# Values sorted as rows and regrouped through DRAM, and one batch's queries turned by the DMA crossbar, in a fused attention and feed-forward kernel

## The chip, the cores and the metric

The kernel runs on one core of a Trainium2 chip. The metric is the device time of one launch in microseconds (us), as a median over runs. TensorE is called PE in the profile, its weight loads PEld, VectorE DVE, ScalarE ACT, GpSimd POOL and SyncE SP. SP computes nothing here: its instructions issue DMAs, and they leave in program order, so an SP instruction that waits holds back every one behind it.

## The reference

Inputs are q, k, v of shape (4 batches, 8 heads, 768 tokens, 64), a block-sorting matrix `sort_net` of (4, 8, 8, 8), two feed-forward weights of 512 x 2048 and 2048 x 512, and two scalars.

```python
P = sort_net
for _ in range(5):
    P = exp(P - max(P)); P /= sum(P, -1) + 1e-9; P /= sum(P, -2) + 1e-9
k_sorted = einsum('bhij,bhjcd->bhicd', P, k_blocks)   # 8 blocks of 96 tokens
v_sorted = einsum('bhij,bhjcd->bhicd', P, v_blocks)
attn = softmax(q_blocks @ k_sorted.T / 8)             # 96 x 96 within each block
x = (attn @ v_sorted) laid out as tokens x 512
h = x @ w_in;  r = relu(h);  out = (s * r * r + b) @ w_out
```

The last division of the Sinkhorn loop is folded into the weights that the kernel builds, and `b` into a bias row.

## The kernel before, in words

The work is cut into eight tiles `t` of 384 tokens, two for each batch `b` (t = 2b and 2b+1). For a tile, `ffn1(t)` makes the hidden layer in eight parts, each of eight products of 384 columns (line L448), a Relu on ACT (L460) and a square on DVE (L461). `ffn2(t)` makes three output tiles, each of sixteen products of 512 columns (L472), scaled and biased on DVE (L493) and stored by SP (L496). This is nearly all of PE's time.

The attention of batch n = b+1 is put between these products in a written order: `ffn1` and `ffn2` take a dictionary of slots, and after part i, or after each four products of an output tile, the pieces in that slot are issued. The schedule is manual, so each engine runs its instructions in program order. The pieces of a batch are, with the names of the lines' helpers:

- `build_pd` (`PDB`): one small product and five DVE operations make PD, the 128 x 128 sorting weights, with a row for each (head, block, half block).
- `k_piece` (`K`): 32 products of 64 columns each sort 16 of 48 key columns into KS (L301).
- `v_piece` (`V`): the same for values. It needs a copy VP of the raw values with the order of token and head dimension exchanged, which `v_sort` makes on POOL in eight copies (L198). Each of four pieces has 32 products of 64 columns (L323), with the slices of VP as weights, and an eviction on DVE or ACT into VS (L204, L206). VS holds a token of a half block on each partition and is what the attention product reads.
- queries: batch 0 and batch 1 are loaded as 64-partition rows (`load_qh`), and turned by transposes on PE (`q_trans`, L217, 48 for a half, evicted by `q_evac`). Batches 2 and 3 are loaded by token (`load_q_rows`, eight DMAs on POOL's queue, L115) and turned by two DMA transposes on SP (`q_dma`, L431).
- `s_piece` (`SC`): scores of four blocks and two heads (L355) and the exponential (L363). The first ones of batch n stand after the first four products of `ffn2(2b+1)`.
- `p_piece` (`P`): the attention product (L397) and its scaling (L403). `t_dma` (`TD`): a DMA transpose on SP to the next tile's input (L423).

Batch 0 goes first on its own path, and the change leaves it alone. The pieces of batch 1 stand in `ffn1(1)`, `ffn2(0)` and `ffn2(1)`, those of batch 2 in `ffn1(2)`, `ffn2(2)` and `ffn2(3)`, and so on. Raw tiles of keys, values and queries have two buffers each. POOL loads the next batch with `load_rest(n)`: six DMAs each of keys and values and eight of queries. `load_rest(2)` is queued on POOL behind `v_sort(1)`; `load_rest(3)` waits, by a one-column copy (L89), for the turned queries of batch 2.

Of the kernel before, what the change touches and what calls it, by code (L numbers as in the profile page):

```python
# [22 lines left out]
def kernel(  # L23
# [40 lines left out]
    xtp = ctx.enter_context(tc.tile_pool(name="xtp", bufs=4))  # L64
    rtp = ctx.enter_context(tc.tile_pool(name="rtp", bufs=3))
    gtp = ctx.enter_context(tc.tile_pool(name="gtp", bufs=2))
    osb = ctx.enter_context(tc.tile_pool(name="osb", bufs=3))
    psa = ctx.enter_context(tc.tile_pool(name="psa", bufs=3, space=bass.MemoryType.PSUM))
    psb = ctx.enter_context(tc.tile_pool(name="psb", bufs=2, space=bass.MemoryType.PSUM))
# [39 lines left out]
    def load_q_rows(b):  # L109

        ti = rawp.tile([BLK, NB, H, D], BF, tag="rawq", name="qtok")
        qv = q[b].rearrange("h (n t) d -> t n h d", n=NB)
        for n in range(0, NB, 2):
            for h in range(2):
                nc.gpsimd.dma_start(out=ti[:, n + h], in_=qv[:, n + h])  # L115
        QTOK[b] = ti

    zeros = const.tile([128, 512], BF)
    nc.vector.memset(zeros, 0.0)  # L119
    VP = [const.tile([128, D, GAP], BF, name=f"vp{i}") for i in range(2)]  # L120
    KS = [const.tile([128, NG, 2, GAP], BF, name=f"ks{i}") for i in range(2)]
    VS = [const.tile([KR, 2 * NG, VW], BF, name=f"vs{i}") for i in range(2)]
    nc.vector.memset(VP[0][:, :, C2:GAP], 0.0)
    nc.vector.memset(KS[0][:, :, :, C2:GAP], 0.0)
    dummy = const.tile([128, 1], FP)
    nc.scalar.activation(out=dummy, in_=zeros[:, 0:1], func=AF.Exp)
# [41 lines left out]
        for a in range(NHP):  # L168
            load_wi(c * W4, (c + 1) * W4, slice(a, a + 1))
    nc.gpsimd.memset(ones, 1.0)  # L170
    nc.gpsimd.memset(VP[1][:, :, C2:GAP], 0.0)
    nc.gpsimd.memset(KS[1][:, :, :, C2:GAP], 0.0)
    fill_vs(1)
    for t, src in ((s_bc, moe_s), (b_bc, moe_b)):
# [3 lines left out]
        nc.gpsimd.dma_start(out=wo[:, fs, :], in_=wov[:, fs, :])  # L178
    for t in "vk":
        load(t, 1, 6)  # L180
    for half in range(2):
        load_qh(1, half)

    rstat = const.tile([BH, NB], FP)
    rrec = const.tile([BH, NB], FP)
# [4 lines left out]
    idv = ident.rearrange("p (a e j z) -> p a e j z", a=NHP, e=2, j=NB)  # L190

    def permute(eng, b, src, cs=slice(0, C2), ds=slice(0, D)):
        o = VP[b % 2][:, ds, cs]
        i = src[:, cs, ds].rearrange("p c d -> p d c")
        if eng is nc.scalar:
            eng.copy(out=o, in_=i)  # L196
        else:
            eng.tensor_copy(out=o, in_=i)  # L198
# [9 lines left out]
    def q_trans(b, half):  # L208
        if b not in QT:
            QT[b] = trp.tile([128, 2, NHP, CQ, 64], BF, tag="qt", name="qt")  # L210
        tr = psa.tile([128, 2, 1024], BF, tag="a", name="tqa")
        pr = slice(half * 64, (half + 1) * 64)
        for a in range(NHP):
            for c in range(CQ):
                for e in range(2):
                    o = (a % 2 * CQ + c) * 64
                    nc.tensor.transpose(out=tr[e * 64:(e + 1) * 64, a // 2, o:o + 64],  # L217
                                        in_=QH[b][pr, 2 * a + e, c, :], identity=ident[pr, pr])
        return tr

    def q_banks(b, half, engs):
        if b not in QT:
# [2 lines left out]
        for u in range(2):  # L225
            tr = psb.tile([128, 1024], BF, tag="b", name="tqb")
            for a in range(2 * u, 2 * u + 2):
                for c in range(CQ):
# [8 lines left out]
    def q_evac(b, half, us, eng, tr):  # L237
        evac(eng, QT[b][:, half].rearrange("p (u a) c t -> p u (a c t)", u=2)[:, us],
             tr[:, us, 0:2 * TG])

    idle = [
        lambda: nc.vector.tensor_reduce(
# [48 lines left out]
            in1=spread(pt, [[0, 4 * NHP], list(pt.ap[1])]), op0=ALU.mult, op1=ALU.mult)  # L291
        PD[b] = pd

    def q_half(b, half, eng):
        q_evac(b, half, slice(0, 2), eng, q_trans(b, half))
# [23 lines left out]
    def v_piece(b, d0, eng, halves=None):  # L319
        ps = psa.tile([128, CK, 2 * NG], FP, tag="a", name="tv")  # L320
        for d in range(CK):
            for z in range(2):
                nc.tensor.matmul(out=ps[z * GAP:(z + 1) * GAP, d, :],  # L323
                                 lhsT=VP[b % 2][:, d0 + d, :], rhs=PD[b][:, :, z, :],
                                 start=True, stop=True)
        if halves is None:
            evac(eng, VS[b % 2][:, :, d0:d0 + CK], ps[0:KR].rearrange("p d g -> p g d"))
            return None

        def half(h, eng):  # L330
            hs = slice(h * HB, (h + 1) * HB)
            evac(eng, VS[b % 2].rearrange("p (g i) w -> p g i w", i=NB)[:, :, hs, d0:d0 + CK],
                 ps[0:KR].rearrange("p d (g i) -> p g i d", i=NB)[:, :, hs])

        half(0, eng)
        return lambda eng: half(1, eng)

    AT = {}
    X = {}
# [186 lines left out]
    part(0, 0, (2,))  # L526
    part(0, 1, (2,))

    def v_sort(b, r=range(8)):
        for i in r:  # L530
            permute(nc.gpsimd, b, RAW["v", b], ds=slice(i * 8, (i + 1) * 8))

    scr = const.tile([128, 1], BF)

    def after(ap):
        nc.gpsimd.tensor_copy(out=scr, in_=ap)  # L536
# [24 lines left out]

    def QF0(): return lambda: q_banks(0, 1, "AD")
    def SB(i): return lambda: s_banks(0, 1, i)
    def QF(b, half, eng): return lambda: q_half(b, half, eng)
    def K(b, i, eng): return lambda: k_piece(b, i * CK, eng)
    def V(b, i, eng): return lambda: v_piece(b, i * CK, eng)
    def SC(b, h, i): return lambda: s_piece(b, h, i)
    def P(b, h, i): return lambda: p_piece(b, h, i)
    def TP(b, h, i, eng): return lambda: t_piece(b, h, i, eng)
    def TD(b, h): return lambda: t_dma(b, h)  # L570
    def PDB(b): return lambda: build_pd(b)
    def LD(t, b): return lambda: load(t, b)


    def halves(n):

        if n == 1:
            s0 = {2: [K(n, 0, "D"), K(n, 1, "A"), K(n, 2, "D")],
                  6: [V(n, 0, "D"), V(n, 1, "A"), V(n, 2, "D")],
                  9: [V(n, 3, "A"), QF(n, 0, "D")], 11: [QF(n, 1, "A")]}  # L580
        else:
            s0 = {0: [K(n, 0, "D"), K(n, 1, "A"), K(n, 2, "D")],
                  8: [V(n, 0, "D"), V(n, 1, "A"), V(n, 2, "D")]}
        s1 = {0: [SC(n, 0, 0), SC(n, 0, 1)] if n == 1 else [V(n, 3, "D"), SC(n, 0, 0), SC(n, 0, 1)],
              3: [P(n, 0, 0), SC(n, 0, 2), SC(n, 0, 3)], 4: [P(n, 0, 1)], 5: [P(n, 0, 2)],
              6: [P(n, 0, 3), TD(n, 0), SC(n, 1, 0), SC(n, 1, 1)], 8: [P(n, 1, 0)],
              9: [P(n, 1, 1), SC(n, 1, 2), SC(n, 1, 3)], 10: [P(n, 1, 2)],
              11: [P(n, 1, 3), TD(n, 1)]}
        return s0, s1
# [5 lines left out]
    part(1, 0, (0, 1))  # L595
    t_piece(0, 1, 3, "D")
    part(1, 1, (0, 1))
    ffn1(1, {2: [PDB(1)], 4: [make_bias]}, {0: 2, 1: 2})
    after(GT[1][:, NF - 1, 0:1])
    v_sort(1)  # L600
    load_rest(2)
    s0, s1 = halves(1)
    ffn2(0, s0)
    ffn2(1, s1)
    for b in range(1, B):
        n = b + 1
        s0, s1 = {}, {}
        if n < B:
            if n == 2:
                v_sort(n)  # L610
            q_dma(n)
            if n == 2:
                load_rest(3, QT[2][:, NB - 1, 0, 0:1])
            s0, s1 = halves(n)
        ffn1(2 * b, {4: [PDB(n)]} if 1 < n < B else {})
        ffn1(2 * b + 1, {})
        if n == 3:
            after(GT[2 * b + 1][:, NF - 1, 0:1])
            v_sort(n)
        ffn2(2 * b, s0)  # L620
        ffn2(2 * b + 1, s1)

# [29 lines left out]
```

## Time and profile before

| What | Value |
|---|---|
| median of 3 runs | 230.36 us (229.96 to 230.58) |
| profiled execution: time, span | 232.06 us, 230.3 us |
| PE busy | 219.7 us, 95% of the span, 2690 matmuls recorded |
| DVE, ACT, POOL busy | 120.6, 100.2, 81.8 us |
| products of `ffn1` and `ffn2` (L448, L472, L485) | 86.6, 81.5, 3.7 us busy |
| value sorting on PE (L323), four batches | 10.4 us busy, 512 products |
| query transposes of batch 1 on PE (L217) | 1.9 us busy, 96 |
| permuting copies on POOL (L198) | 19.1 us busy, 24 copies |

A line of the groups names the source line, engine and operation, what is written from what, the shape and the count; then the busy time, the mean of one in ns, and the idle time before the group with what ended it. Matmuls overlap, so that the mean of one (326 ns for 384 columns) is longer than the step from one to the next (86.6 us / 512 = 169 ns). The chain of waits is the path that ended last, followed back from the last instruction; its rows have the start, the length, and what ran.

### The profile page before, as it was taken

The numbers are of one execution on the slowest core, as the hardware profiler recorded it, in microseconds if no ns is written. First come the engines' busy times: TensorE is split into PE (matmuls) and PEld (weight loads), VectorE is DVE, ScalarE is ACT, GpSimd is POOL, SyncE is SP. The second block draws the span as 40 slices with busy tenths as digits, with TensorE's granted clock in tenths as the row PEclk, the third lists the DMA queues.
The fourth block names the chain that finished last, engine by engine and source line by source line (L and its number), as shares of the span: only waits on it lengthen the run. The fifth ranks groups of instructions, "written<-read, shape, count | busy, mean of one in ns | idle before, by whom it ended". The sixth has DMA issues, their size and how long they took to land.

```text
span 230.3 us, 6164 instructions
## 1 busy us (share of the span) xinstructions
PE 219.7 (95%) x2690; PEld 134.4 (58%) x2713; DVE 120.6 (52%) x237; ACT 100.2 (43%) x135; POOL 81.8 (36%) x139
## 2 busy tenths in 40 slices
PE   7978999899999999999999999999999999999994
PEld 5767766456555555666465655565555566554453
DVE  6684457377642774546255765446365664432221
ACT  4785687443215436565015245663033446660000
POOL 7569991267987860469000000005500000000000
PEclk9997999999999999999999999999999999999999
DMA  6999989998199969499912238000111440001112
GB/s 153 277 158 132 128 125 197 205 200 134 51 140 229 179 143 183 73 145 177 110 48 91 70 114 188 0 3 3 66 74 46 117 114 3 1 0 48 72 64 93
DMA packets 45883, 25.05 MB, mean 109 GB/s; under 512 B 29984, under 2 KB 42016, under 8 KB 45856
## 3 DMA queue, kind: packets, MB, share of 16 engines
q0 software_dynamic: 25952, 12.85, 43.9%
q1 hardware_dynamic: 19904, 11.81, 18.5%
q8 instruction: 21, 0.34, 0.6%
q14 instruction: 6, 0.05, 0.1%
HBM read 27.27 MB, written 6.29 MB: 146 GB/s over the span
## 4 chain that ended last, share of the span: by engine, by line
PE 89%; DMA 4%; ACT 2%; issue 2%; SPq 1%; DVE 1%
PE hps L448 37%; PE ops L472 34%; DMA v0f<-in_v_dram 4%; PE tv L323 4%; PE pv L397 4%; PE sc L355 2%; PE tp L301 2%; PE ops L485 2%; PE scb L373 1%; PE tqa L217 1%; PE pv L391 1%; ACT vp L196 1%; SPq L80 1%; PE tr L414 1%; PE pe L276 0%
## 5 line engine op out<-in xcount | busy, mean ns | idle before, releaser
L448 PE MATMUL hps<-xt,wi 128*128 128x384 bf16 x512 | 86.6, 326 | 1.3 <-DVE xt L206 1.3
L472 PE MATMUL ops<-wo,gt 128*128 128x512 bf16 x346 | 81.5, 379 | 2.2 <-issue 1.6
L460 ACT ACTIVATE rt<-hps 128x768 bf16<-128x768 f32 x64 | 51.8, 810 | 39.9 <-PE hps L448 39.3
L448 PEld LDWEIGHTS <-wi 128*128 128x128 bf16 x512 | 48.8, 98 | 33.2 <-issue 1.9
L461 DVE TENSOR_TENSOR gt<-rt 128x768 bf16<-128x768 bf16 x64 | 36.4, 570 | 45.2 <-ACT rt L460 44.9
L472 PEld LDWEIGHTS <-gt 128*128 128x128 bf16 x368 | 33.6, 98 | 36.8
L493 DVE SCALAR_TENSOR_TENSOR ot<-ops,s_bc,bias 128x512 f32<-128x512 f32 (+1 forms) x25 | 18.2, 729 | 36.3 <-PE ops L472 34.1
L403 DVE TENSOR_TENSOR x<-pv,rec 96x512 bf16<-96x512 f32 x32 | 22.0, 687 | 1.1
L363 ACT ACTIVATE at<-sc 112x768 bf16<-112x768 f32 x16 | 12.1, 807 | 21.0 <-PE sc L355 21.0
L198 POOL COPY vp<-rawv 128x384 bf16<-128x384 bf16 x24 | 19.1, 859 | 0.0
L536 POOL COPY scr<-gt 128x1 bf16<-128x1 bf16 x2 | 0.4, 190 | 48.1 <-DVE gt L461 48.0
L397 PEld LDWEIGHTS <-at 112*128 112x128 bf16 (+1 forms) x256 | 13.4, 102 | 6.7 <-ACT at L363 0.6
L204 ACT CAST vs<-tv 112x1024 bf16<-112x1024 f32 (+1 forms) x7 | 6.3, 898 | 23.3 <-PE tv L323 23.2
L206 DVE CAST vs<-tv 112x1024 bf16<-112x1024 f32 (+1 forms) x11 | 12.0, 1122 | 7.3 <-PE tv L323 7.3
L141 POOL DMA_DIRECT2D wi<-in_moe_w_in_dram x24 | 12.9, 566 | 4.7 <-DMA qh<-in_q_dram 2.6
L397 PE MATMUL pv<-vs,at 112*128 112x66 bf16 (+1 forms) x256 | 14.1, 197 | 0.0
L115 POOL DMA_DIRECT2D qtok<-in_q_dram x16 | 12.3, 775 | 2.3 <-PE sc L355 1.0
L92 POOL DMA_DIRECT2D rawk<-in_k_dram x21 | 11.3, 552 | 4.9 <-DMA wo<-in_moe_w_out_dram 4.1
L92 POOL DMA_DIRECT2D rawv<-in_v_dram x18 | 9.7, 578 | 7.7 <-DMA wo<-in_moe_w_out_dram 4.8
L323 PEld LDWEIGHTS <-vp 128*64 128x64 bf16 x512 | 9.4, 117 | 2.9 <-issue 2.1
L131 PE MATMUL z<-zeros 128*64 128x96 bf16 (+2 forms) x129 | 9.8, 242 | 1.3 <-DVE zeros L119 1.2
L206 DVE CAST ks<-tp 128x1024 bf16<-128x1024 f32 x8 | 9.5, 1220 | 2.1 <-PE tp L301 2.0
(83 smaller groups left out, 147.8 us busy)
## 6 DMA issues: line engine op xcount, KB each, us to landing
out_dram<-ot SPq DMA_DIRECT2D x23, 256.0 KB, 2.0
rawv<-in_v_dram POOLq DMA_DIRECT2D x18, 128.0 KB, 6.6
rawk<-in_k_dram POOLq DMA_DIRECT2D x18, 128.0 KB, 5.1
wo<-in_moe_w_out_dram POOLq DMA_DIRECT2D x4, 512.0 KB, 10.4
v0f<-in_v_dram SPq DMA_DIRECT2D x4, 384.0 KB, 7.1
qtok<-in_q_dram POOLq DMA_DIRECT2D x16, 96.0 KB, 4.6
qh<-in_q_dram POOLq DMA_DIRECT2D x3, 384.0 KB, 7.7
wi<-in_moe_w_in_dram POOLq DMA_DIRECT2D x16, 64.0 KB, 3.8
```

The costliest lines, as they stand in the source:

```text
L92: nc.gpsimd.dma_start(out=ti[:, c:c + n, :].rearrange("p c d -> p (c d)"), in_=raw["qkv".index(t)][b][:, c * D:(c + n) * D])
L141: nc.gpsimd.dma_start(out=wi[:, al, f0:f1], in_=wiv[:, al, f0:f1])
L198: eng.tensor_copy(out=o, in_=i)
L206: nc.vector.tensor_copy(out=out, in_=in_)
L323: nc.tensor.matmul(out=ps[z * GAP:(z + 1) * GAP, d, :], lhsT=VP[b % 2][:, d0 + d, :], rhs=PD[b][:, :, z, :], start=True, stop=True)
L397: nc.tensor.matmul(out=pv[0:m, e, n * VW:(n + 1) * VW], lhsT=atf[:, c0:c0 + m], rhs=VS[b % 2][:, e * NG + g0 + n, :], start=True, stop=True)
L403: nc.vector.tensor_tensor(out=x[:, :, hp * 128:(hp + 1) * 128].rearrange("p n (e d) -> p e n d", e=2), in0=pvv[:, :, :, 0:D], in1=rec.unsq ...
L448: nc.tensor.matmul(out=H1[t, i][:, f, 0:TG], lhsT=wi[:, hp, fc:fc + 128], rhs=XT[t][:, :, hp, :], start=(hp == 0), stop=(hp == NHP - 1))
L460: nc.scalar.activation(out=rt, in_=h, func=AF.Relu)
L461: nc.vector.tensor_tensor(out=gt[:, 2 * i:2 * i + 2, :], in0=rt, in1=rt, op=ALU.mult)
L472: nc.tensor.matmul(out=ops, lhsT=gt[:, f, m * 128:(m + 1) * 128], rhs=wo[:, f, :], start=(f == 0), stop=(f == NF - 1))
L493: nc.vector.scalar_tensor_tensor(out=ot[:, ns], in0=ops, scalar=s_bc, in1=BIAS[0][:, ns], op0=ALU.mult, op1=ALU.add)
```

## The change

For batches 1 to 3, the values are sorted as they were loaded: PD is the weight, and the 3072 raw columns (48 tokens x 64) go through in six products of 512 columns (`v_rows`, `VRW`). Each is evicted in place over the raw values by DVE ("D") or ACT ("A"). The sorted rows then have a (parity of head, half block, head pair and block) on each partition and have to be regrouped: `v_back` (`VB`) writes them to DRAM in one DMA (128 rows of 6 KB), and four DMAs read them back into VS in runs of 64 values, one run for each of 48 tokens and 32 groups. All five go through SP's queue. The permuted copies, their buffer VP[1] and the later `v_piece` calls go.

The queries of batch 1 are loaded by token with eight DMAs and turned by two DMA transposes on SP, behind `v_back(1)`. `load_rest(2)` now waits for both of them. PD of batch 1 is built two parts earlier, that of batches 2 and 3 one part earlier. In program order on SP, batch 1 has: a small fill of VS, the write, the four reads, the two query transposes, and then the stores of tile 0; batches 2 and 3 have the two query transposes, the write and four reads, and then the stores of the next tile.

```diff
-    VP = [const.tile([128, D, GAP], BF, name=f"vp{i}") for i in range(2)]
+    VP = const.tile([128, D, GAP], BF, name="vp")
...
-    for half in range(2):
-        load_qh(1, half)
+    load_q_rows(1)
...
+    def v_rows(b, u, eng):
+        w = 512 // D
+        r = RAW["v", b][:, u * w:(u + 1) * w, :].rearrange("p c d -> p (c d)")
+        ps = psb.tile([128, 512], FP, tag="b", name="tvr")
+        nc.tensor.matmul(out=ps, lhsT=PD[b].rearrange("p e z g -> p (e z g)"), rhs=r,
+                         start=True, stop=True)
+        evac(eng, r, ps)
+
+    def v_back(b):
+        vd = drp.tile([2, 2, NG, C2, D], BF, tag="vd", name="vd")
+        nc.sync.dma_start(out=vd.rearrange("e z g c d -> (e z g) (c d)"),
+                          in_=RAW["v", b].rearrange("p c d -> p (c d)"))
+        for z in range(2):
+            for e in range(2):
+                nc.sync.dma_start(
+                    out=VS[b % 2][z * GAP:z * GAP + C2, e * NG:(e + 1) * NG, 0:D],
+                    in_=vd[e, z].rearrange("g c d -> c g d"))
...
-        if n == 1:
-            s0 = {2: [K(n, 0, "D"), K(n, 1, "A"), K(n, 2, "D")],
-                  6: [V(n, 0, "D"), V(n, 1, "A"), V(n, 2, "D")],
-                  9: [V(n, 3, "A"), QF(n, 0, "D")], 11: [QF(n, 1, "A")]}
-        else:
-            s0 = {0: [K(n, 0, "D"), K(n, 1, "A"), K(n, 2, "D")],
-                  8: [V(n, 0, "D"), V(n, 1, "A"), V(n, 2, "D")]}
-        s1 = {0: [SC(n, 0, 0), SC(n, 0, 1)] if n == 1 else [V(n, 3, "D"), SC(n, 0, 0), SC(n, 0, 1)],
+        s0 = {2 if n == 1 else 0: [K(n, 0, "D"), K(n, 1, "A"), K(n, 2, "D")]}
+        s1 = {0: [SC(n, 0, 0), SC(n, 0, 1)],
...
-    ffn1(1, {2: [PDB(1)], 4: [make_bias]}, {0: 2, 1: 2})
-    after(GT[1][:, NF - 1, 0:1])
-    v_sort(1)
-    load_rest(2)
+    ffn1(1, {0: [PDB(1)], 2: [VRW(1, 0, "D")], 3: [VRW(1, 1, "A")], 4: [make_bias, VRW(1, 2, "A")],
+             5: [VRW(1, 3, "D")], 6: [VRW(1, 4, "A")], 7: [VRW(1, 5, "D")]}, {0: 2, 1: 2})
+    nc.sync.dma_start(out=VS[1][C2:GAP, :, 0:D],
+                      in_=spread(zeros[0:GAP - C2, 0:D], [[0, 2 * NG], [1, D]]))
+    v_back(1)
+    q_dma(1)
+    load_rest(2, QT[1][:, NB - 1, 0, 0:1])
...
         if n < B:
-            if n == 2:
-                v_sort(n)
             q_dma(n)
             if n == 2:
                 load_rest(3, QT[2][:, NB - 1, 0, 0:1])
             s0, s1 = halves(n)
-        ffn1(2 * b, {4: [PDB(n)]} if 1 < n < B else {})
-        ffn1(2 * b + 1, {})
-        if n == 3:
-            after(GT[2 * b + 1][:, NF - 1, 0:1])
-            v_sort(n)
+            u0 = {3: [PDB(n)], 5: [VRW(n, 0, "D")], 6: [VRW(n, 1, "D")], 7: [VRW(n, 2, "D")]}
+            u1 = {0: [VRW(n, 3, "D")], 1: [VRW(n, 4, "D")], 2: [VRW(n, 5, "D"), VB(n)]}
+        ffn1(2 * b, u0)
+        ffn1(2 * b + 1, u1)
```

More of the change, by code (lines that the diff above doesn't have):

```diff
@@ L66 @@
     gtp = ctx.enter_context(tc.tile_pool(name="gtp", bufs=2))
+    drp = ctx.enter_context(tc.tile_pool(name="drp", bufs=2, space=bass.MemoryType.DRAM))
     osb = ctx.enter_context(tc.tile_pool(name="osb", bufs=3))
@@ L119 @@
     nc.vector.memset(zeros, 0.0)
-    VP = [const.tile([128, D, GAP], BF, name=f"vp{i}") for i in range(2)]
+    VP = const.tile([128, D, GAP], BF, name="vp")
     KS = [const.tile([128, NG, 2, GAP], BF, name=f"ks{i}") for i in range(2)]
     VS = [const.tile([KR, 2 * NG, VW], BF, name=f"vs{i}") for i in range(2)]
-    nc.vector.memset(VP[0][:, :, C2:GAP], 0.0)
+    nc.vector.memset(VP[:, :, C2:GAP], 0.0)
     nc.vector.memset(KS[0][:, :, :, C2:GAP], 0.0)
@@ L170 @@
     nc.gpsimd.memset(ones, 1.0)
-    nc.gpsimd.memset(VP[1][:, :, C2:GAP], 0.0)
     nc.gpsimd.memset(KS[1][:, :, :, C2:GAP], 0.0)
@@ L192, in permute @@
     def permute(eng, b, src, cs=slice(0, C2), ds=slice(0, D)):
-        o = VP[b % 2][:, ds, cs]
+        o = VP[:, ds, cs]
         i = src[:, cs, ds].rearrange("p c d -> p d c")
@@ L206, in evac @@
             nc.vector.tensor_copy(out=out, in_=in_)
[L208 to L219, printed above, removed]
     def q_banks(b, half, engs):
@@ L235, in q_banks @@
                  tr[:, 0:2 * TG])
-    def q_evac(b, half, us, eng, tr):
-        evac(eng, QT[b][:, half].rearrange("p (u a) c t -> p u (a c t)", u=2)[:, us],
-             tr[:, us, 0:2 * TG])
     idle = [
@@ L292, in build_pd @@
         PD[b] = pd
-    def q_half(b, half, eng):
-        q_evac(b, half, slice(0, 2), eng, q_trans(b, half))
     def k_piece(b, c0, eng):
@@ L323, in v_piece @@
                 nc.tensor.matmul(out=ps[z * GAP:(z + 1) * GAP, d, :],
-                                 lhsT=VP[b % 2][:, d0 + d, :], rhs=PD[b][:, :, z, :],
+                                 lhsT=VP[:, d0 + d, :], rhs=PD[b][:, :, z, :],
                                  start=True, stop=True)
@@ L527 @@
     part(0, 1, (2,))
[L529 to L536, printed above, removed]
     def load_rest(b, behind=None):
@@ L563, in SB @@
     def SB(i): return lambda: s_banks(0, 1, i)
-    def QF(b, half, eng): return lambda: q_half(b, half, eng)
     def K(b, i, eng): return lambda: k_piece(b, i * CK, eng)
-    def V(b, i, eng): return lambda: v_piece(b, i * CK, eng)
     def SC(b, h, i): return lambda: s_piece(b, h, i)
@@ L569, in TP, with VRW, VB @@
     def TP(b, h, i, eng): return lambda: t_piece(b, h, i, eng)
+    def VRW(b, u, eng): return lambda: v_rows(b, u, eng)
+    def VB(b): return lambda: v_back(b)
     def TD(b, h): return lambda: t_dma(b, h)
     def PDB(b): return lambda: build_pd(b)
-    def LD(t, b): return lambda: load(t, b)
     def halves(n):
-        if n == 1:
-            s0 = {2: [K(n, 0, "D"), K(n, 1, "A"), K(n, 2, "D")],
-                  6: [V(n, 0, "D"), V(n, 1, "A"), V(n, 2, "D")],
-                  9: [V(n, 3, "A"), QF(n, 0, "D")], 11: [QF(n, 1, "A")]}
-        else:
-            s0 = {0: [K(n, 0, "D"), K(n, 1, "A"), K(n, 2, "D")],
-                  8: [V(n, 0, "D"), V(n, 1, "A"), V(n, 2, "D")]}
-        s1 = {0: [SC(n, 0, 0), SC(n, 0, 1)] if n == 1 else [V(n, 3, "D"), SC(n, 0, 0), SC(n, 0, 1)],
+        s0 = {2 if n == 1 else 0: [K(n, 0, "D"), K(n, 1, "A"), K(n, 2, "D")]}
+        s1 = {0: [SC(n, 0, 0), SC(n, 0, 1)],
               3: [P(n, 0, 0), SC(n, 0, 2), SC(n, 0, 3)], 4: [P(n, 0, 1)], 5: [P(n, 0, 2)],
@@ L606 @@
         n = b + 1
-        s0, s1 = {}, {}
+        s0, s1, u0, u1 = {}, {}, {}, {}
         if n < B:
-            if n == 2:
-                v_sort(n)
             q_dma(n)
```

## The prediction

> **What bounds the kernel now.** I read the page first: its slices and the chain by engine.
>
> ```profile
> PE   7978999899999999999999999999999999999994
> ...
> PEclk9997999999999999999999999999999999999999
> DMA  6999989998199969499912238000111440001112
> ...
> PE 89%; DMA 4%; ACT 2%; issue 2%; SPq 1%; DVE 1%
> ```
>
> PE is busy in every slice after the first 25 us, and 89% of the path that ended last is PE itself. So PE work that goes shortens the time one for one, as long as nothing that PE needs comes late. The DMA row has room only in places: full to slice 20 but for slice 10 (58 to 63 us), lighter after it.
>
> Then the chain in order of time, between `ffn2(0)` and the first scores of batch 1:
>
> ```profile
> 53.50 2.54 PE ops L472 x11
> ...
> 61.23 1.64 PE tv L323 x96
> 62.87 0.16 issue
> ...
> 65.57 0.62 PE tv L323 x32
> 66.19 0.88 PE tqa L217 x48
> 67.07 0.16 issue
> 67.23 1.68 PE ops L472 x7
> 68.90 0.87 PE tqa L217 x48
> ...
> 70.75 0.45 PE sc L355 x16
> ```
>
> Value sorting and query transposes stand on the path themselves, with a gap of 0.16 us where PE goes back to the large products.
>
> **What PE saves.** Batch 1: 1.64 + 0.16 + 0.62 + 0.88 + 0.16 + 0.87 = 4.33 us. The rows of batches 2 and 3 give 1.64 + 0.16 + 0.63 and 1.64 + 0.16 + 0.62. Together 9.18 us. Added are 18 products of 512 columns. The 80 such products at the end of the chain (`ffn2(6)` and two tiles of `ffn2(7)`, 206.40 to 223.62) step by 0.215 us, so 3.87 us. Net **-5.31 us**. DVE and ACT lose eleven evictions of some 1 us and two of queries, and get 18 of 128x512 from PSUM (0.55 to 0.75 us each: the 128x768 query eviction and the 128x512 output row L493). A part of `ffn1` takes 1.5 us with such a product in it, and Relu (0.81) and square (0.57) lie on different engines, so these evictions stay covered: nothing on the path (uncovered, 18 x 0.65 = 12 us). POOL's 19.1 us of copies were on no path: nothing.
>
> **PD of batch 1.** It is asked for after part 2 of `ffn1(1)`, on PE at 45.40 + 0.36 = 45.76. The five DVE operations took 46.75 to 48.00, 1.25 us. They now follow the squares that end at 45.58 at the latest, or 44.95 if only the first is ahead; I take the second, as the written order has it: 46.2. PE waits **+0.45 us** (0 to 1.1). The raw values land at 46.06 to 49.2 (issue plus landing of the six), one behind the other, before each product wants them. Behind that wait on PE stand the rest of `ffn1(1)` and all that follows. So `ffn2(0)` starts at T0 = 53.45 + 0.45 + 6 x 0.215 = 55.2. Batches 2 and 3 have PD early by two parts: nothing.
>
> **The new chain on SP, batch 1.** The scores waited for a transpose on PE; now they wait for a line of DMAs:
>
> ```profile
> out_dram<-ot SPq DMA_DIRECT2D x23, 256.0 KB, 2.0
> ...
> qtok<-in_q_dram POOLq DMA_DIRECT2D x16, 96.0 KB, 4.6
> ...
> qt<-qtok SPq DMA_TRANSPOSE x4, 4.6
> ```
>
> Issue to landing in us is the last number. (1) The last sorted chunk is evicted by DVE behind the bias operations (3.1 us), two squares and a chunk: about 56.9. (2) The write of 786 KB: a 256 KB store lands in 2.0 us, of which 0.7 is data (DMA share 0.35 in a window of 2 us); three times the data, 1.3 + 2.1 = 3.4 us, to 60.4. Under load stores took up to 6.0. Here the eight query loads are nearly done: the last keys land at 53.7, and loads of this kind moved 2338 packets in the 2 us from 108 to 110. (3) The four reads: 6144 runs of 128 bytes, 384 on each of 16 DMA engines. No row has this operation. Bounds: those query loads, also runs of 128 bytes written from DRAM, went at 2 us x 16 / 2338 = 13.7 ns each per engine, 5.3 us for all four; but their share was 231%, so one packet takes 31.6 ns, and one at a time would be 12.1 us. Three crossbar transposes (1536 pieces of 256 bytes each, from SP's queue, share 101%) took 137.75 to 143.0, 1.77 us each; four of these are 7.1 us. I take 6.2, between the nearest two. With 1.2 us from issue to first data, as that transpose shows (136.58 to 137.75), the data end at 60.4 + 1.2 + 6.2 = 67.8. (4) The transposes stand behind them in the queue: 1.77 of data and 0.75 to the landing (3.7 us in all after issue): the first half of the queries is there at 70.3.
>
> The scores want it at T0 + (70.75 - 53.50) - 4.33 = 68.1. PE waits **+2.2 us**: none if the reads take under 4.0 us, 8.1 if 12.1. The values themselves are wanted 3.7 us after the scores and are there by 69. Behind the waiting scores PE has the rest of `ffn2(1)`; nothing else can run. On SP the three stores of `ffn2(0)` are behind the transposes; output buffers are three, the fourth is wanted after 72, and the first store lands about 74: PSUM's second buffer covers that.
>
> **The clock.** A waiting PE costs more than the wait, as the windows show:
>
> ```profile
> 17.00:18.00 1.00, 0.02 (x2) 0.00 (x0) 0.46 (x1) 0.87 (x2) 1.00 (x3) 1.00 1.02 123
> 18.00:19.00 1.00, 0.67 (x26) 0.59 (x27) 0.00 (x0) 0.32 (x1) 1.00 (x3) 0.88 0.93 115
> 19.00:20.00 1.00, 1.00 (x46) 1.00 (x44) 0.43 (x1) 0.49 (x1) 1.00 (x3) 0.50 1.06 126
> ```
>
> The third number from the end is the granted clock. Waits of 0.56 and 1.31 us close together were followed by 3.4 us at half clock (18.75 to 22.16), worth up to 1.7 us of PE work. A wait of 2.2 us may do this or not: I put **+0.8 us** (0 to 1.7). The Trainium skill ("TensorE: Matmul & The Clock Gate", Why this matters for your kernels) tells one to avoid idle gaps over about 3 us; by that rule a 2.2 us wait would be free, and the sum would be 0.8 lower. The row, with less idle time than that, speaks against the rule's bound, and I go by the row.
>
> Another rule speaks against the change: "DMA: Bandwidth & Descriptors", Specifications, asks for at least 512 bytes per transfer for line rate. An estimate from it, 6144 runs charged as 512 bytes each (3.1 MB) at a store's 374 GB/s, is 8.4 us for the reads, and the sum would be 2.2 us higher. The crossbar row shows 256-byte pieces at 18 ns, cheaper than that, so it is not a term here.
>
> **Later batches.** `load_rest(2)` started at 62.24 and its last query landed at 82.2; now it starts at 72 (second transpose) and ends at 92. `ffn1(2)` starts near 85, and its first row product at 93, when all values (13 us after the start of the loads) are there: nothing. `q_dma(2)` goes out at 92 instead of 87.6; queries 2 are wanted after 120: nothing. `v_back(2)` waits for DVE at about 102 and then runs beside `load_rest(3)` (98 to 116), with some 3 us to spare before the attention product at 124: nothing in the forecast, a rival below. Batch 3 has no loads beside it and 20 us: nothing.
>
> **Sum.** Against the profiled execution, -5.31 + 0.45 + 2.2 + 0.8 = -1.86 us: span 228.4 and time 230.2 instead of 232.06 (1.8 us lie around the span). That execution was 1.70 us above the median of the runs, so I apply the difference to the median: 230.36 - 1.86 = 228.5.
>
> **The rivals.**
>
> *All transfers hidden.* If the reads run at 13.7 ns per run or less and are issued without gaps, with the loads 1 us early because POOL has one fill less, the wait is under 1 us, and no clock is lost. 230.36 - 5.31 + 0.45 = 225.5. For it: DMA slices are empty from 56 to 63. Against: it needs every link of a chain of three landings at its lower bound. 0.13.
>
> *The reads take the wait.* One mechanism: a run of 128 bytes is a packet of its own, on SP's queue one at a time. At 31.6 ns the four take 12.1 us, PE waits 8.1 us at the first scores of batch 1 and loses 1.2 of clock: 230.36 - 5.31 + 0.45 + 8.1 + 1.2 = 234.8, slower. It decides from a read time of about 7.6 us (1.9 us each), where wait and clock reach 4.9. For it: transposes in the same queue show one packet at a time. Against: these moved twice the bytes per packet in 18 ns. 0.22.
>
> *A second wait in batch 2.* As forecast for batch 1, but the round trip of batch 2 lies among `load_rest(3)`, where a store landed in 4.9 to 5.6 us instead of 2.0, and query packets fill the engines. With the write at 8 and the reads at 12 us the values land near 126, 2 us late at the attention product, and a clock loss may follow: 228.5 + 2 to 4, so 230.5 to 232.5. 0.15.
>
> That the change doesn't do what it says I leave out: the instructions are on the queues as it says.
>
> **How the numbers follow.** The forecast, waits of 1 to 4 us in batch 1, has 0.50 and gives 226.5 to 230.0. Measurement tells 0.3% (0.7 us) from no change. Faster: 0.44 of the forecast and the first rival, 0.57. Same: 0.06 and 0.07 of the batch 2 rival, 0.13. Slower: 0.22 and 0.08, 0.30. The range goes from the first rival, 225.3, to 234.0, most of the second: signs differ, and the forecast's own range is 226.5 to 230.0.
>
> **What would show it.** Right: PE busy 5 us less; the first L355 scores of batch 1 wait some 2 us for the turned queries; reads landing 6 to 8 us after the write; the clock row with one more dip near 70 us; `load_rest(2)` starting at 72. Wrong: no PE idle time at these scores (then the first rival), over 5 us there (the second), or a wait at the first attention product of batch 2 (the third).

## The result and the profile after

The changed kernel takes 242.24 us (median of 5 runs, 241.51 to 245.01) against 230.39 us (229.96 to 230.71): a ratio of 1.0521, 95% interval 1.0487 to 1.0554. It is 11.9 us slower, where 1.9 us faster was forecast, and outside the range. The profiled execution took 242.26 us with a span of 240.5 us (before 232.06 and 230.3). Lines of before are 3 higher than the same lines of after in the loops: L355 is now L352, L448 is L445, L472 is L469.

The slices and the chain by engine, from the page of after:

```profile
PE   8969997899938975999999899999999999999994
...
PEclk9997999999985995899999999999999999999999
DMA  6999999999999999949999755803971343001112
...
PE 78%; DMA 11%; SPq 4%; DVE 2%; ACT 2%; issue 1%
```

A slice is 6.0 us, and the first is slice 0. PE has a hole at slice 11 (66 to 72 us) and another at slices 14 and 15 (84 to 96 us); behind the early dip at slice 3, which before has too, the clock row dips twice more, at slices 11-12 and 15-16. PE's share of the path fell from 89 to 78%; DMA and SP's queue went from 5 to 15%. The waits of PE between 40 and 140 us (engine, line, what it waited for; total, times, longest):

```profile
PE sc L352 <- DMA qt<-qtok: 4.6, 1, 4.6
PE hps L445 <- DMA xt<-x: 3.8, 1, 3.8
PE hps L445 <- DVE xt L205: 1.3, 1, 1.3
PE pv L394 <- DMA vs<-vd: 0.9, 2, 0.5
PE tvr L321 <- DVE gt L458: 0.7, 1, 0.7
```

Before had the third alone. The first was forecast at 2.2, the last at 0.45; the second, for the input of the third tile, was not forecast. The chain in order of time (start, length, what ran) shows what stands behind the first two, and behind the values of batch 2:

```profile
57.09 3.53 DMA vd<-rawv
...
60.63 0.33 SPq L331
...
61.01 0.77 SPq L331
...
61.82 1.28 SPq L331
...
63.15 2.25 SPq L331
...
65.58 7.15 DMA qt<-qtok
...
72.87 0.82 PE sc L352 x16
...
83.35 9.30 DMA xt<-x
...
92.70 2.42 PE hps L445 x7
```

The write starts and lands as forecast (56.9 and 60.4 forecast). Then each of the four reads holds SP longer than the one before, and the transposes behind them land at 72.7 and not at 70.3. The second is new: the DMA transpose to `ffn1(2)`'s input lands after 9.3 us; before it took 4.2.

The windows show the clock (third number from the end) at each wait:

```profile
70.00:71.00 1.00, 0.00 (x0) 0.00 (x0) 0.00 (x0) 0.00 (x0) 0.00 (x0) 0.70 1.49 66
...
74.00:75.00 1.00, 1.00 (x4) 0.42 (x3) 0.00 (x0) 0.92 (x2) 0.60 (x2) 0.50 1.00 381
...
91.00:92.00 1.00, 0.00 (x0) 0.00 (x0) 0.00 (x0) 0.00 (x0) 0.00 (x0) 0.50 2.02 175
...
95.00:96.00 1.00, 1.00 (x5) 0.49 (x4) 0.00 (x0) 0.52 (x1) 0.00 (x0) 0.50 1.45 208
```

The clock is at half from 70.4 to 77.2 and from 90.9 to 97.7, 6.8 us each. PE works in the later part of both (72.87 to 77.2, 92.7 to 97.7) and loses about half of it, 2.2 and 2.5 us. The account of the span: 230.3 - 5.31 (PE work, as costed) + 0.68 + 4.64 + 2.2 + 3.83 + 2.5 + 0.9 = 239.7, measured 240.5. The spans differ by 10.2 us and the medians by 11.9, since the profiled execution of before lies 1.7 us above its median and that of after on it; both had half clock from 19 to 22 us. So this account covers the 10.2 us.

### The profile page after: what moved, and what is told of

It reads as the page before. It is cut to its first block, busy times and chain, and to the rows that moved or that the text cites. A ratio compares the mean times of both kernels' runs of the same rounds, so it can differ in the third digit from the quotient of the medians.

```text
span 240.5 us, 5296 instructions
## 1 busy us (share of the span) xinstructions
PE 222.2 (92%) x2251; PEld 130.0 (54%) x2251; DVE 118.5 (49%) x243; ACT 96.4 (40%) x133; POOL 66.4 (28%) x119
## 4 chain that ended last, share of the span: by engine, by line
PE 78%; DMA 11%; SPq 4%; DVE 2%; ACT 2%; issue 1%
PE hps L445 35%; PE ops L469 24%; SPq L331 4%; PE z L132 4%; DMA xt<-x 4%; PE pv L394 3%; DMA qt<-qtok 3%; DMA vs<-vd 3%; PE sc L352 2%; PE tp L280 2%; PE tvr L321 2%; DMA vd<-rawv 1%; PE ops L482 1%; ACT rt L457 1%; PE scb L370 1%
## 5 line engine op out<-in xcount | busy, mean ns | idle before, releaser
L445 PE MATMUL hps<-xt,wi 128*128 128x384 bf16 x512 | 91.6, 332 | 5.1 <-DMA xt<-x 3.8
L469 PE MATMUL ops<-wo,gt 128*128 128x512 bf16 x368 | 86.4, 385 | 0.0
L445 PEld LDWEIGHTS <-wi 128*128 128x128 bf16 x512 | 49.7, 99 | 39.3 <-issue 4.0
L469 PEld LDWEIGHTS <-gt 128*128 128x128 bf16 x368 | 34.6, 99 | 39.3 <-issue 2.6
L360 ACT ACTIVATE at<-sc 112x768 bf16<-112x768 f32 x24 | 18.1, 806 | 56.7 <-PE sc L352 56.7
L116 POOL DMA_DIRECT2D qtok<-in_q_dram x24 | 18.4, 775 | 4.5 <-issue 2.4
L352 PE MATMUL sc<-qt,ks 64*128 64x96 bf16 x200 | 7.0, 209 | 5.9 <-DMA qt<-qtok 4.6
L205 DVE CAST rawv<-tvr 128x512 bf16<-128x512 f32 x15 | 10.3, 684 | 0.0
L399 DVE RECIPROCAL rec<-pv 96x8 f32<-96x8 f32 x32 | 6.4, 201 | 7.0 <-PE pv L394 6.9
L132 PEld LDWEIGHTS <-zeros 128*64 128x64 bf16 (+1 forms) x130 | 7.8, 118 | 3.0 <-DVE zeros L120 1.2
```

What stands on the lines that cost most here:

```text
L132: nc.tensor.matmul(out=z[0:m, 0:w], lhsT=zeros[:, 0:m], rhs=zeros[:, 0:w], start=True, stop=True)
L360: nc.scalar.activation(out=at, in_=sc[0:KR, :, 0:TG], func=AF.Exp, scale=scale)
L445: nc.tensor.matmul(out=H1[t, i][:, f, 0:TG], lhsT=wi[:, hp, fc:fc + 128], rhs=XT[t][:, :, hp, :], start=(hp == 0), stop=(hp == NHP - 1))
L469: nc.tensor.matmul(out=ops, lhsT=gt[:, f, m * 128:(m + 1) * 128], rhs=wo[:, f, :], start=(f == 0), stop=(f == NF - 1))
```

## The experiments

The theory after the result: the loss is two waits with a clock dip each. One comes from the reads in short runs, the other from `load_rest(2)`, which starts at 74 us and not 62, and so runs beside the DMA transposes of batch 1. Rivals: the crossbar queries alone cost it; the round trips of batches 2 and 3 cost it; the clock alone; the short runs of the query loads. All times are medians against before on the same chip (230.2 to 230.9).

**Parts of the change by themselves.** First, the kernel before with batch 1's queries through the crossbar and nothing else:

```diff
-    for half in range(2):
-        load_qh(1, half)
+    load_q_rows(1)
...
     v_sort(1)
+    q_dma(1)
```

> The kernel before with one part of the change alone: batch 1's queries loaded by token and turned by the crossbar, values of all batches still sorted on PE. Theory A (the reads of 128-byte runs ahead of the transposes in SP's queue made the queries late): without reads ahead of them the turned queries land near 63 us, before the scores want them at 68.7, nothing waits, and PE loses 1.75 + 0.32 us of transposes: 228.3 us. Rival B (eight loads of queries by token on POOL's queue are themselves too slow for batch 1): the scores of batch 1 wait for the turned queries, 232 us or more.

Measured 237.83 us (233.67 to 238.01, four runs; too wide for a ratio); the profiled run is the fastest, 233.67. It is over 232, but for a cause that no theory had named: the queries came in time, and their eight loads hold POOL for 6.2 us (batch 1's own query loads before: 1.4), so the permuting copies behind them start at 58.0 instead of 55.9, and PE waits for them five times 0.34 us, with a clock dip from 63.6 to 67.0. A wait of 0.9 us for the third tile's transpose is there too. A repeat, after it was clear that this transpose is the place to look at:

> The first experiment's kernel once more (batch 1's queries by crossbar alone), since its runs gave 233.7 and 238 us and only the first was profiled. Theory L (the eight query loads keep POOL 6.2 us, the permuting copies start 2 us late, PE waits 1.7 us for them in small pieces; whether the clock dips there once or more sets the rest): in a run of 238 us there is a second dip or a wait over 2 us at the third tile's input. Rival: one long wait at batch 1's scores.

Measured 235.06 us (232.82 to 235.10), ratio 1.0183 (1.0133 to 1.0233). Its profile has a wait of 2.9 us at the third tile (the transpose took 8.3 us) and none for POOL. So even without the DRAM trip, a PE that is early meets the loads. What decides between these waits from run to run stays open, and the runs of 238 us were not traced.

Next, row sorting and the DRAM trip in batches 2 and 3 only; batch 1 as before:

```diff
-            s0 = {0: [K(n, 0, "D"), K(n, 1, "A"), K(n, 2, "D")],
-                  8: [V(n, 0, "D"), V(n, 1, "A"), V(n, 2, "D")]}
+            s0 = {0: [K(n, 0, "D"), K(n, 1, "A"), K(n, 2, "D")]}
...
+            u0 = {3: [PDB(n)], 5: [VRW(n, 0, "D")], 6: [VRW(n, 1, "D")], 7: [VRW(n, 2, "D")]}
+            u1 = {0: [VRW(n, 3, "D")], 1: [VRW(n, 4, "D")], 2: [VRW(n, 5, "D"), VB(n)]}
```

> The kernel before with the row products and the trip through DRAM for batches 2 and 3 alone; batch 1 as before. Theory A: the trip fits where nothing is queued behind it: PE loses 2.43 + 2.42 and gets 12 x 0.216 = 2.6 us, 228.1 us, with a wait of at most 1 us at the first attention product of batch 2. Rival C (the trip through DRAM costs waits wherever it stands): 231 us or more, with waits in both batches.

228.82 us, ratio 0.9933 (0.9914 to 0.9951): faster than both kernels. From its page:

```profile
PE 219.2 (97%) x2469; PEld 131.0 (58%) x2469; DVE 120.4 (53%) x243; ACT 98.0 (43%) x133; POOL 68.8 (30%) x122
...
PE   7988998999999999999999999999999999999993
...
PEclk9999999999999999999999999999999999999999
```

No hole and full clock: the round trip of batch 2 is hidden, but only just. The write goes out at 101.05, the reads from 108.06 on, and the last read, its issue with the time to landing, and the first attention product of batch 2 are:

```profile
115.35 1.71 SPq L353 DMA_DIRECT2D vs<-vd  x1
...
vs<-vd SPq DMA_DIRECT2D x1, 192.0 KB, 6.3
...
121.81 0.27 PE pv L416 x8
```

The values land at 121.7 and PE starts on them at 121.8 without a wait. So the loss lies in batch 1's part, and batch 2's part has some 0.1 us to spare in this execution.

Then both, with batch 1's loads and slots reordered so that the queries' POOL time is early (row values stay in batches 2 and 3, batch 1's queries by crossbar):

```diff
-    for t in "vk":
-        load(t, 1, 6)
-    for half in range(2):
-        load_qh(1, half)
+    load("v", 1, 6)
+    load_q_rows(1)
+    load("k", 1, 6)
...
-            s0 = {2: [K(n, 0, "D"), K(n, 1, "A"), K(n, 2, "D")],
-                  6: [V(n, 0, "D"), V(n, 1, "A"), V(n, 2, "D")],
-                  9: [V(n, 3, "A"), QF(n, 0, "D")], 11: [QF(n, 1, "A")]}
+            s0 = {4: [K(n, 0, "D"), K(n, 1, "A"), K(n, 2, "D")],
+                  7: [V(n, 0, "D"), V(n, 1, "A"), V(n, 2, "D")],
+                  10: [V(n, 3, "A")]}
```

> A version meant to be faster: rows and the trip through DRAM for batches 2 and 3 alone, and batch 1's queries by crossbar with their loads ahead of batch 1's keys, the key pieces two slots later and the value pieces one. By the single terms: 228.8 - 2.07 + 0.5 = 227.2 us. If POOL's permuting copies are late again, 231 us or more.

232.94 us (230.32 to 236.60), ratio 1.0059 (1.0018 to 1.0100): PE waits 2.8 us for the raw keys, which now come last. The crossbar queries bring nothing here.

**The clock alone.** Products of zeros fill both waits, 20 before the first scores of batch 1 and 17 before `ffn1(2)`:

```diff
+            nc.tensor.matmul(out=z, lhsT=zeros[:, 0:128], rhs=zeros, start=True, stop=True)
...
-        s1 = {0: [SC(n, 0, 0), SC(n, 0, 1)],
+        s1 = {0: ([FL(20)] if n == 1 else []) + [SC(n, 0, 0), SC(n, 0, 1)],
```

> The changed kernel with 20 products of zeros on PE before the first scores of batch 1 and 17 before the third feed-forward tile, where PE stands idle for 4.6 and 3.8 us; nothing else is different. Theory A: the two dips of the clock after the waits (6.8 us each at half) cost PE 2.3 and 2.7 us; with PE kept busy the clock stays full and the time is 237.3 us, the waits themselves staying. Rival D (the waits set the time and PE would have waited anyhow, the clock only goes along): 242 us.

242.12 us, ratio 1.0509 (1.0490 to 1.0529): no gain. But the clock stayed full through both waits, and `ffn2(2)` started at 112.6 instead of 117.7. The time was given back later, as the clock row of its page and the group of the attention products show (the last number is the idle time and what ended it):

```profile
PEclk9999999999999999999999799999999999999999
...
L394 PE MATMUL pv<-vs,at 112*128 112x66 bf16 (+1 forms) x256 | 14.3, 197 | 3.8 <-DMA vs<-vd 3.8
```

The chain of the same kernel, up to that product:

```profile
108.11 8.24 DMA vd<-rawv
...
117.93 5.07 SPq L331
...
123.05 9.86 DMA vs<-vd
...
132.95 0.31 PE pv L394 x4
```

PE is early and meets the next late transfer, batch 2's values, whose trip lies among `load_rest(3)`: 25 us from write to landing. PE is not what sets the time here; a chain of DMAs is: queries of batch 1, loads of batch 2, its transposes, loads of batch 3, values of batch 2. The clock's 5 us are no cause that can be taken out alone.

**The reads.** Batch 1's four reads bring the same bytes in runs of 6 KB, to a scratch tile. The kernel leaves the regrouping out: zeros, filled by POOL instead of SP's small fill, stand for batch 1's sorted values.

```diff
+                    nc.sync.dma_start(out=scr[r:r + NG],
+                                      in_=vd[e, z].rearrange("g c d -> g (c d)"))
```

> The changed kernel, but in batch 1 alone the four reads bring the same bytes from DRAM in runs of 6 KB into a scratch tile, and the sorted values of batch 1 are left out (zeros stand in their place). Theory A: run length, not bytes or the round trip, makes the reads slow: their data take some 2 us instead of 9, the queries land near 65 us and the first wait of 4.6 us and its clock dip go; the wait for the next tile's input remains in part: 235.3 us. Rival E (the trip itself, write then read, is what is slow): the scores still wait over 3 us and the time is 240 us or more.

240.22 us (two runs), ratio 1.0433 (1.0405 to 1.0462). The reads land 3.6 us after issue, SP issues the four in 2.0 us instead of 4.8, and the scores wait for nothing: from the start of the write to the landing of the first turned queries it is 10.4 us (59.28 to 69.7) where after has 15.6. The run length makes the first wait. The total missed (some 235 expected): PE also waited 2.5 us for batch 1's raw values at the first row product and 2.5 us at batch 2's first attention products, and the second wait grew to 5.4 us, as its chain shows:

```profile
77.90 0.54 PE ops L477 x3
78.44 10.83 DMA xt<-x
...
89.31 5.72 PE hps L453 x18
```

The transpose goes out 4.9 us earlier than in after, and lands only 3.4 us earlier.

**When the loads of batch 2 start.** In the changed kernel, the query loads of batch 2 wait for the second transpose of batch 1's output:

```diff
+        if b != 2:
+            load_q_rows(b)
...
     ffn2(1, s1)
+    load_q_rows(2, XT[3][0:BLK, HB - 1, NHP - 1, BLK - 1:BLK])
```

> The changed kernel, but batch 2's eight query loads are issued only after the second DMA transpose of batch 1's attention output has landed, so that they no longer run beside these transposes. Theory H (one serial chain of DMAs, turned queries 1, loads 2, transposes and queries 2, loads 3, values 2; whatever wait of PE is relieved, the next link takes it up): the wait for the third tile's input (3.8 us) and its clock dip go, but loads 3 start no earlier and the values of batch 2 are waited for longer, 3 to 4 us: 238 to 240 us. Rival F (independent waits, each gives its time back): 242.2 - 3.8 - 2.7 = 235.7 us.

240.96 us, ratio 1.0475 (1.0406 to 1.0543), a little over the 238 to 240 expected. The transposes land in 5.0 and 3.9 us and the wait at the third tile is gone; in its place PE waits 3.2 us for batch 2's values beside 4.3 at the first scores, as in after. PE waits 2.0 us for the raw values too. Again the next link takes the gain.

The loads not gated at all, as in the kernel before:

```diff
-    load_rest(2, QT[1][:, NB - 1, 0, 0:1])
+    load_rest(2)
```

> The changed kernel, but the loads of batch 2 are issued at once behind the bias copies on POOL (57 us) and no longer wait for batch 1's turned queries. Theory H: the later links run as early as in the kernel before, so no wait at the third tile's input and none at the values of batch 2; but write and reads of batch 1 now share the DMA engines with these loads, and the first wait grows from 4.6 to some 10 us: 236 to 239 us. Rival F: the first wait stays and the others go: 242.2 - 6.5 - 0.9 = 234.8 us.

245.41 us, ratio 1.0636 (1.0578 to 1.0693), above the expected 236 to 239. Now the reads of batch 1 run beside the loads, and SP needs 13.2 us to issue them. From the page:

```profile
PEclk9999999999985579999999999999999999999999
...
L352 PE MATMUL sc<-qt,ks 64*128 64x96 bf16 x200 | 7.0, 209 | 16.1 <-DMA qt<-qtok 15.3
```

A wait of 15.3 us, half again what was expected; the transposes to the third tile, by now without loads beside them, land in 3.9 and 4.1 us.

Row values in all batches, but batch 1's queries turned on PE as before, with the loads of batch 2 ungated in one kernel and behind the last read in the other:

```diff
-    load_q_rows(1)
+    for half in range(2):
+        load_qh(1, half)
...
-    q_dma(1)
-    load_rest(2, QT[1][:, NB - 1, 0, 0:1])
+    load_rest(2)        # the other: load_rest(2, VS[1][GAP:KR, 2 * NG - 1, 0:1])
```

> The changed kernel with batch 1's queries loaded and turned on PE as before; the loads of batch 2 at once (57 us). The values of all three batches go through DRAM. Theory H: nothing is queued behind the reads, but reads and loads share the engines, the values of batch 1 land near 78 us instead of the 73.6 where they are wanted: a wait of about 5 us with a clock dip at the first attention product, none later: 234 to 236 us. Rival J (only the transposes behind the reads were at fault): 230.4 - 2.3 - 2.43 + 1.3 + 0.7 = 227.7 us.

> As the run with batch 1's queries turned on PE and all values through DRAM, but the loads of batch 2 wait for the last read of batch 1's values. Theory H: no wait at batch 1's scores and at most 1 us at its values, but loads 2 start near 72 us as in the changed kernel, so the third tile's input is late by 4 to 6 us with a clock dip, and the values of batch 2 after it: 234 to 237 us. Rival J: 227.7 us.

Both came out slower than expected (234 to 236 and 234 to 237). Ungated: 242.06 us, 1.0486 (1.0426 to 1.0546); the last values land at 81.9 and not near 78, and PE waits 6.7 and 1.6 us at the attention product, with a dip of 10.2 us and no wait at the third tile. Behind the reads: 238.82 us, 1.0344 (1.0296 to 1.0392); no wait at the scores, but 5.2 us at the third tile, whose transposes take 10.7 and 9.9 us. Of the places for `load_rest(2)` that were tried, each collides: early with the reads, late with the transposes.

**Is it the query loads' short runs?** Queries of batch 2 loaded as rows of 1 KB, which leaves them in another order:

```diff
+            for n in range(NB):
+                nc.gpsimd.dma_start(out=ti[:, n].rearrange("p h d -> p (h d)"),
+                                    in_=qf[:, n * w:(n + 1) * w])
```

> The changed kernel, but batch 2's queries are loaded as flat rows of 1 KB (96 runs to a DMA instead of 768, the same bytes and the same eight DMAs), so that batch 2's queries are in a wrong order. Theory H: the query loads of 128-byte runs are what holds up the DMA transposes of batch 1's output; with long runs the wait at the third tile (3.8 us) and its dip go, queries 2 and loads 3 come earlier, and the values of batch 2 are not waited for: 242.2 - 6.5 - 0.9 = 234.8 us. Rival K (any load of batch 2 at that place holds them up, whatever its runs): the third tile still waits over 2 us, 239 us or more.

243.60 us, 1.0557 (1.0501 to 1.0614). In the profiled run, the longest of the four (245.97), the wait at the third tile is 7.6 us, and the transposes take 13.1 and 13.0 us. With this and the long reads together:

> Both short-run costs taken out of batch 1's surroundings: batch 2's queries as flat rows of 1 KB, and batch 1's four reads as runs of 6 KB into a scratch tile (batch 1's sorted values left out). Theory H: then none of PE's long waits is left and the change gives what PE saves: 230.4 - 5.3 + 0.7 + 0.5 = 226.3 us (to 228 if the early wait for raw values is long again). Rival K: the waits come back elsewhere, over 231 us.

239.47 us, 1.0371 (1.0302 to 1.0441), where 226.3 was expected from short runs as the cause; the transposes take 13.3 and 15.0 us, and the wait is

```profile
PE hps L461 <- DMA xt<-x: 7.8, 1, 7.8
```

Short runs in the loads are not what holds the transposes up; loads in rows of 1 KB do so too.

**The transposes taken away.** Batch 1's output is turned by products on PE, as batch 0's is, in the changed kernel and in the one with long reads:

```diff
-              6: [P(n, 0, 3), TD(n, 0), SC(n, 1, 0), SC(n, 1, 1)], 8: [P(n, 1, 0)],
+              6: [P(n, 0, 3)] + ([] if n == 1 else [TD(n, 0)]) + [SC(n, 1, 0), SC(n, 1, 1)], 8: [P(n, 1, 0)],
...
+            s1[7] = [TP(1, 0, hp, "AD"[hp % 2]) for hp in range(NHP)]
...
+                u0[hp] = [TP(1, 1, hp, "A")] + u0.get(hp, [])
```

> The changed kernel, but batch 1's attention output is turned by PE transposes with evictions on ACT and DVE (32 transposes, 1.4 us, and about 1 us of small waits) instead of two DMA transposes; the loads of batch 2 stand as in the changed kernel. Theory M (the victims are DMA transposes that run beside loads, whatever the loads' runs are): no wait at the third tile and no second dip: 242.2 - 6.5 + 2.4 = 238.1 us, or up to 240 if the values of batch 2 are then waited for longer. Rival N (the third tile waits for something else that the late loads hold up): the wait of 3.8 us stays, 244 us.

> The same on top of the run with batch 1's four reads in runs of 6 KB (batch 1's sorted values left out). Theory M: both long waits are gone, 240.2 - 5.4 - 2.7 + 2.4 = 234.5 us, with what is left at the values of batch 2 and in the early wait for raw values. Rival N: 240 us or more.

The first: 237.46 us, 1.0269 (1.0201 to 1.0337), near the expected 238.1. The wait at the third tile and its dip are gone, and `ffn1(2)` starts at 90.9; the first wait and one dip stay, in the clock row and the group of the scores:

```profile
PEclk9999999999997999999999999999999999999999
...
L352 PE MATMUL sc<-qt,ks 64*128 64x96 bf16 x200 | 7.0, 209 | 5.0 <-DMA qt<-qtok 4.7
```

The second: 231.01 us (229.70 to 232.92, ten runs), 1.0008 (0.9975 to 1.0042), better than expected, with full clock and one wait left:

```profile
PEclk9999999999999999999999999999999999999999
...
L321 PE MATMUL tvr<-rawv,pd 128*128 128x512 bf16 x18 | 6.8, 379 | 2.4 <-DMA rawv<-in_v_dram 2.4
```

With both waits taken away the 11.9 us are gone. What holds this kernel at the time of before is in its trace: the PE transposes take 2.7 us of the chain, 0.9 of them in waits for their evictions, and 2.4 us go to the raw values at the first row product; -5.31 + 2.7 + 2.4 = -0.2 us, measured +0.2 (-0.6 to +1.0).

## Why the prediction was wrong, step by step

**What PE saves: right.** Its busy time rose (219.7 to 222.2 us), since work at half clock takes longer, so the busy row I named as a test could not show it. The lag between the two traces does: over batch 3, with no wait in either, after gains 1.07 us, where 2.42 - 1.29 = 1.13 was costed. In the kernel with rows in batches 2 and 3, the measured gain of 1.5 us (1.1 to 2.0) is somewhat short of the 2.27 that the same terms give.

**PD, T0, the last sorted chunk, the write: right.** 0.68 us (0.45 forecast), 55.1 (55.2), 57.0 (56.9), landing at 60.6 (60.4).

**The raw values: right by luck.** The prediction has them "before each product wants them". In the profiled execution of after, which has the early dip of the clock, the first raw values landed at 46.0, 0.1 us before the first row product. Of the nine experiments with batch 1's row products whose trace has no early dip, eight waited 1.0 to 2.5 us there for them (the ninth waited 1.5 us for DVE). So this term was put at nothing with no margin, and it is one of those that hold the last experiment at the time of before.

**The reads: mis-sized.** This is the first step that failed, point 3 of the new chain, "I take 6.2, between the nearest two". The DMA answer for 57 to 73 us (40 slices of 0.4 us) has the trip in one row:

```profile
GB/s 79 27 343 399 476 369 369 56 0 0 0 38 166 199 94 115 98 90 72 71 81 94 101 107 96 94 100 101 86 75 103 110 114 93 17 285 289 283 200 290
```

The write is the block at some 400 GB/s, the reads the stretch from 61.4 to 70.7, at 70 to 115 after its first microsecond, and the transposes come back at 285. That is 9.3 us, 24 ns for a run of 128 bytes on an engine, not 16. The crossbar's 18 ns for 256 bytes was no guide to it. Here the Trainium skill ("DMA: Bandwidth & Descriptors", Specifications) was nearer: charging each run as 512 bytes, the estimate that the prediction weighed and dropped, gave 8.4 us. I had set it aside for a row of another kind of DMA. So the wait was 4.64 and not 2.2 us; the second rival had this mechanism, at 12.1 us, with 7.6 as the point from which it decides. The measured trip was between the two. (The stated range begins at 225.3, where the first rival's own sum gives 225.5.)

**The clock: mis-sized, and too few.** "+0.8 us (0 to 1.7)" stood for one wait of 2.2 us. Two waits each brought 6.8 us at half clock, worth 2.2 and 2.5. The Trainium skill ("TensorE: Matmul & The Clock Gate", Why this matters for your kernels) names gaps over about 3 us; both waits were longer, and fit. Five waits of 0.34 us in the first experiment, which brought 3.4 us at half, do not, and neither does the wait of 3.2 us with deferred queries, which brought none.

**Later batches: the step that failed outright.** The text has `load_rest(2)` "starts at 72 ... and ends at 92", and asks of values and queries alone whether they come late: "nothing". It starts at 74, and the last query load, issued at 89.2, lands at 101.5 (before: 81.8, where the prediction reads 82.2). The prediction never asked what else runs in that time. `t_dma(1, 0)` and `t_dma(1, 1)` do, and they and the loads slow each other. Two stretches of after, and two of before, show the queues (q0 the loads, q1 SP's) with packets, MB and share. After, from 84 to 87 us, which starts 0.7 us after the first transpose was issued:

```profile
q0 software_dynamic: 928, 0.53, 129.8%
q1 hardware_dynamic: 71, 0.03, 4.1%
```

Beside the loads of the values it moves next to nothing. After, from 89 to 91 us, beside the query loads:

```profile
q1 hardware_dynamic: 779, 0.20, 93.0%
...
q0 software_dynamic: 726, 0.09, 83.9%
```

The counts are as if the two queues took turns, one packet each, some 376 per us on each, at 146 GB/s together. Alone, in the trace of before, query loads had (75 to 77 us):

```profile
q0 software_dynamic: 2338, 0.31, 233.6%
```

And crossbar transposes alone, also in before (87 to 90 us):

```profile
q1 hardware_dynamic: 2545, 0.64, 91.9%
```

That is 1169 and 848 packets per us. A tile's transpose, 393 KB in packets of 256 bytes or 1536 of them, so takes 4 us beside the loads and not 1.8, after the stretch in which it gets none; 9.3 us in all, and PE waits 3.83. Equal turns are not the rule, though: beside the rows of 1 KB, from 88 to 94 us of that kernel, it was 1371 packets on q1 and 255 on q0 in 6 us, and the transposes had still fewer packets per us (229). The times to landing go with the loads beside them:

| Loads of batch 2 | The two transposes, issue to landing, us |
|---|---|
| before; rows in batches 2 and 3 (early) | 4.2, 3.6; 4.4, 3.6 |
| crossbar queries alone, first and second run (last load landed 4.9 and 8.7 us after the first transpose went out) | 6.3, 4.5; 8.3, 5.3 |
| the same with rows, reordered (2.5 us after) | 4.0, 4.0 |
| ungated; with PE queries (early) | 3.9, 4.1; 4.0, 5.5 |
| queries deferred | 5.0, 3.9 |
| after; with fill | 9.3, 11.4; 9.4, 9.5 |
| long reads; behind the last read | 10.8, 11.6; 10.7, 9.9 |
| 1 KB rows; with long reads | 13.1, 13.0; 13.3, 15.0 |

The hint stood in the trace of before: its transpose at 79.1 met the last query loads until 81.8 and landed at 83.3, one of 4.2 us where the next took 3.6.

**The third rival** was right in its place and too strong in its price: batch 2's values came late by 0.9 us, because PE itself was 11 us late by then. Where PE was earlier (fill, deferred queries), the wait was 3.2 to 3.8 us, and with rows in batches 2 and 3 alone there was none, by 0.1 us.

**The method** failed in one more way: the terms were added as if independent. The gate that makes `load_rest(2)` wait ties the transfers into one chain, and the experiments show that a wait taken out of it alone comes back at the next link. Only with two links cut did the time return.

## What to carry to other kernels

When a change delays a block of loads, list every DMA that other code issues inside its new window, and ask of each when it is wanted: here two crossbar transposes, untouched by the change, took 9.3 and 11.4 us instead of 4.2 and 3.6. Price a transfer of a new kind by its own kind of run, and when no row has it, let the dearer bound set the forecast if PE has nothing else to do behind it. Take the part of a change whose chain is still hidden (here the later batches: 0.9933 of the time before), check how much slack it has left, and leave the part whose chain has none.

## What the runs showed of the hardware

- Query loads from POOL's queue and crossbar transposes from SP's together moved less than either alone: 146 GB/s with runs of 128 bytes (89 to 91 us of after) and 96 with rows of 1 KB (88 to 94 us of that kernel), against 156 for the loads and 214 for the transposes alone. Why a packet of one holds up a packet of the other was not tried.
- SP is held at the issue of a DMA of 1536 runs: 0.33, 0.77, 1.28, 2.25 us for four in a row, 13.2 us in all beside loads; four in runs of 6 KB take 2.0 us.
- POOL is held 0.77 us for the issue of each query load of 768 runs, against 0.55 for a load of keys; with eight of them ahead, the permuting copies started 2.1 us later.
- Every dip of the clock in these traces lasted a multiple of 3.41 us: 6.8 us for waits of 3.8, 4.3, 4.6, 5.2 and 5.4 us, 10.2 us for 6.7 and 7.8, and 17.1 us for 15.3. The length of the wait alone does not set it: one of 4.7 us brought 3.4, waits of 2.2 and 2.5 us brought 3.4, and waits of 2.0, 2.4, 2.9 and 3.2 us brought none. Products of zeros in two of the waits kept the clock full.
